# Newton steps of the spectral norms, and two row splits, written for GpSimd instead of VectorE, in a two-layer FNet and sliding-window attention kernel

## The chip, the cores and the metric

The kernel runs on one core of one Trainium2 chip. The metric is the device time of one execution in microseconds (us), the median of the runs; a lower time is better. PE is TensorE (matmuls), DVE is VectorE, ACT is ScalarE, POOL is GpSimd, SP is the engine that issues most transfers.

## The reference

Four sublayers are applied in turn to a sequence of 2048 rows of 640 numbers: spectral mixing, attention, spectral mixing, attention. Each adds to its input what it computes from the normed input.

```python
x = x + _A_ref(_layernorm(x), dft_seq_re, dft_seq_im, dft_hid_re, dft_hid_im)
x = x + _B_ref(_layernorm(x), wqkv, wo)
...
def _A_ref(x, ...):
    a = jnp.einsum("bsd,ed->bse", x, dft_hid_re)
    b = jnp.einsum("bsd,ed->bse", x, dft_hid_im)
    return jnp.einsum("ts,bse->bte", dft_seq_re, a) - jnp.einsum("ts,bse->bte", dft_seq_im, b)
```

`_B_ref` is attention with 32 heads of 20 and a window of 256 rows, with a projection to q, k and v before it and one after it. `_layernorm` takes the mean off a row and divides by the root of its variance plus 1e-5; it has no weights.

## The kernel before

**Layers and tiles.** The 2048 rows are 16 tiles of 128. `spectral` and `attention` are called once for each of the two layers, spectral first. Numbers for TensorE are kept as two 16-bit floats, a high half and the low half that is left (`hi` and `lo`), and a product is made of three matmuls (high by high, high by low, low by high).

**The spectral sublayer.** Its sequence transform is done in 4 rounds r of 4 row tiles, each of 8 steps j. Before a round, four "z stages" (`z_stage`) transform the round's four row tiles along the hidden axis; they are spread over the steps of the round before. A step j makes the seven products of a Strassen form, in the order m0 (bank x, `main_a`), then m6 (bank z) and m5 (bank y) of the step before (`main_c`), then m1 (y), m2 (x), m4 (z) and m3 (y) (`main_b`). A product is 12 matmuls. DVE adds the result of a product to the residual tiles (`add`, L559); the second product in a PSUM bank (m3 after m1, m6 after m4, m5 after m3) can begin only when DVE has read what the first left there. POOL adds the parts that are shared by two residual quarters: L579 after m0, L589 after m1, L600 after m3. For the next step, `take_c` makes four sums of the matrix's quarters on POOL (L525 to L528), ACT makes seven high halves (L533) and DVE the seven low halves (L536).

**Norms.** `norm_steps` norms a list of row tiles: two BN_STATS and a BN_AGGR a tile give mean and variance (L139, L142), L148 and L149 make a first guess of the inverse root, three Newton steps refine it (L151, L152, two instructions of one number a row each), and with `act` L156 makes the bias and ACT the normed row (L164). Then a split makes the high half on ACT (L177) and the low half (L178) on the engine that is given. In `spectral` norms stand in two places. `side_norm` norms one row tile for a later z stage, 12 tiles a layer, with its split on POOL. `finish(0, 1)` and `finish(1, 1)` norm the first two pairs of row tiles for the attention that follows, near the end of the last round, with their splits on DVE; the normed rows of a pair are transposed by TensorE (four groups of five, `transposed`, copied out by ACT and by DVE in turn), and the projections of the first pair are made among the last products of the round (`ahead`).

**What sets the order.** These norms are generators: `tick`, which is called after every product, runs the next pair of high and low halves and then one step of each generator to its next `yield`. A scheduler then orders every engine's instructions by the order of the program and by when it reckons that their inputs and buffers are free; each engine works through its own list in that order. Matmuls have two banks for x, y, z and for `pf` (transposes, projections), the sums of the matrix three buffers.

```python
            def tick(cut=True):
                if splits and cut:
                    with behind():
                        for f in splits.pop(0):
                            f()
                with behind():
                    for g in list(side):
                        if next(g, None) is None:
                            side.remove(g)
```

Of the kernel before, what the change touches and what calls it, by code (L numbers as in the profile page):

```python
# [13 lines left out]
I32 = mybir.dt.int32  # L14
AF = mybir.ActivationFunctionType
OP = mybir.AluOpType
# [38 lines left out]
ROOT = float(0x5F3759DF - (1 << 22) - (1 << 30))  # L55
# [8 lines left out]
X_UP = 2.0 ** 10  # L64
# [8 lines left out]
def body(ctx: ExitStack, tc: tile.TileContext, x_in, cmat, whid, wqkv, wo, out):  # L73
    nc = tc.nc
# [42 lines left out]
    normed = [None]  # L117
# [11 lines left out]

    matmul, transpose = partial(tensor, "matmul"), partial(tensor, "transpose")  # L130

    def norm_steps(xs, ys, act=False):

        n = len(xs)
        mv = keep.tile([P, n, 2], F32, tag=f"lnmv{n}", name="lnmv", bufs=2)
        for k, x in enumerate(xs):
            st = keep.tile([P, 2, 6], F32, tag="lnst", name="lnst", bufs=2)
            for h in range(2):
                nc.vector.bn_stats(st[:, h], x[:, h * 320:(h + 1) * 320])  # L139
                if h == 0:  # L140
                    yield
            nc.vector.bn_aggr(mv[:, k], st.rearrange("p a b -> p (a b)"))  # L142
            yield
        t = keep.tile([P, 3, n], F32, tag=f"lnt{n}", name="lnt", bufs=2)
        ts = nc.vector.tensor_scalar
        for k in range(n):
            h, g, u = (t[:, m, k:k + 1] for m in range(3))
            ts(h, mv[:, k, 1:2], 1e-5, -0.5 * X_UP ** -2, op0=OP.add, op1=OP.mult)  # L148
            ts(g.bitcast(I32), h.bitcast(I32), -0.5, ROOT, op0=OP.mult, op1=OP.add)  # L149
            for m in range(3):  # L150
                ts(u, g, g, h, op0=OP.mult, op1=OP.mult)  # L151
                normed[0] = ts(g, u, 1.5, g, op0=OP.add, op1=OP.mult).ins  # L152
                if m == 0:
                    yield
            if act:
                normed[0] = ts(u, mv[:, k, 0:1], g, -1.0, op0=OP.mult, op1=OP.mult).ins  # L156
            yield
        for _ in range(2 if act else 0):
            yield
        for k, x in enumerate(xs):  # L160
            g, u = t[:, 1, k:k + 1], t[:, 2, k:k + 1]
            y = keep.tile([P, D], F32, tag="lny", name="lny", bufs=2)
            if act:
                nc.scalar.activation(y, x, AF.Identity, bias=u, scale=g)  # L164
            else:
                normed[0] = ts(y, x, mv[:, k, 0:1], g, op0=OP.subtract, op1=OP.mult).ins
            ys.append(y)
            yield

    def layer_norm(xs):  # L170
        ys = []
        for _ in norm_steps(xs, ys):
            pass
        return ys

    def split(hi, lo, y, eng):
        nc.scalar.activation(hi, y, AF.Copy)  # L177
        eng.tensor_tensor(lo, y, hi, op=OP.subtract)  # L178
# [3 lines left out]
    def load(out, in_):  # L182
        with ExitStack() as order:
            if in_turn[0] and loads:
                order.enter_context(tc.issue_after(loads[-1]))
            elif floor:
                order.enter_context(tc.issue_after(floor[-1]))
            i = nc.sync.dma_start(out, in_)
        loads.append(i.ins)
# [189 lines left out]
    def spectral(layer, res_src, hidden, first):  # L379
        with ExitStack() as st:  # L380
# [47 lines left out]
            def transposed(xs, k, xt):  # L428
                pt = new_f().bitcast(F16)[:, :ND * P].rearrange("p (a b) -> p a b", a=ND)
                for dt in range(ND):  # L430
                    transpose(pt[:, dt], xs[:, k, dt * P:(dt + 1) * P], idh)
                if k:
                    nc.vector.tensor_copy(xt[:, k], pt)
                else:
                    nc.scalar.activation(xt[:, k], pt, AF.Copy)
# [3 lines left out]
            def load_x(s):  # L439
                x = sb.tile([P, D], F32, tag="xin", name="xin", bufs=NXIN)  # L440
                load(x, res_src[s])
                return x

            def split_x(s, y, eng):
                XS[s] = keep.tile([P, 2, D], F16, tag="xs", name="xs", bufs=2)
                split(XS[s][:, 0], XS[s][:, 1], y, eng)
# [36 lines left out]
            def side_norm(s):  # L483
                x, ys = load_x(s), []
                for _ in range(3):
                    yield 1
                for _ in norm_steps([x], ys, True):
                    yield 1
                split_x(s, ys[0], nc.gpsimd)
                yield 1  # L490
# [140 lines left out]
            def finish(j, pace):  # L631
                xs = [sb.tile([P, D], F32, tag="xin", name="x2", bufs=NXIN) for k in range(2)]
                for k in range(2):
                    load(xs[k], x2_d[2 * j + k])
                for _ in range(3):
                    yield 1
                ys, xss = [], []
                for _ in norm_steps(xs, ys, True):
                    for _ in range(pace):
                        yield 1  # L640
                for y in ys:
                    xs = keep.tile([P, 2, D], F16, tag="xs", name="xs", bufs=2)
                    split(xs[:, 0], xs[:, 1], y, nc.vector)
                    xss.append(xs)
                    yield 1
                for _ in range(2):
                    yield 1
                proj.new_rows(j)
                for k, xs in enumerate(xss):
                    for m in range(2):  # L650
                        transposed(xs, m, proj.rows[j][0][:, k])
                        yield 1
                    finished[0] += 1
# [79 lines left out]
            if first:  # L733
                constants()
                x = [load_x(s) for s in range(2)]
                f = [load_w(n) for n in range(NXIN - 2)]
                norm_x(0, x[:1], nc.vector)
                for n in range(10):
# [5 lines left out]
                    if n == 7:  # L744
                        x = [load_x(s) for s in range(2, 4)]
# [3 lines left out]
            for r in range(NR):  # L749
                for k in range(RS if r == 0 else 0):  # L750
                    s = RS * r + k
                    if first:
                        if s == 1:
                            norm_x(2, x, nc.gpsimd)
                            marks["dve"] = normed[0]
                        if s:
                            turned_x(s)
                        if k < RS - 1:
                            turn_x(s + 1, 2)
                    elif s > 1:  # L760
                        hidden.fetch(s)
                    if r == 0 and k == 1:
                        load_c(1)
                        with behind() as order:
                            if not first:
                                order.enter_context(tc.issue_after(hidden.after))
                            take_c(0)
                    if first and k == RS - 1:
                        side.append(side_norm(RS))
                    if first or s > 1:  # L770
                        z_stage(s)
                if r == NR - 1:
                    proj = Projections()
                for j in range(NJ):
                    n = r * NJ + j
# [35 lines left out]
                    if r < NR - 1 and j in STAGES[r]:  # L811
                        k = STAGES[r].index(j)
# [629 lines left out]
```

## Time and profile before

| what | value |
|---|---|
| median of 3 runs | 2056.11 us (2054.0 to 2058.06) |
| profiled execution, its own time | 2055.16 us |
| span of its profile | 2053.4 us |
| PE busy | 1987.5 us (97%) |
| DVE busy | 1563.3 us (76%) |
| POOL busy | 1469.2 us (72%) |
| ACT busy | 1115.0 us (54%) |
| granted TensorE clock, mean | 0.996 of full speed |

The span is that of the instructions; 1.76 us of the execution's own time lie around it. The first spectral layer takes about the first 555 us of it, the second about 1060 to 1565 us; the attention layers follow each. In a row of the timeline stand start, duration, engine, line, operation, output<-inputs, shape, count, and in brackets the engine's idle time before the row with what ended it; rows of equal neighbours are merged and overlap their successor by the pipeline's tail. In a row of the waits stand total, times and longest, in us.

### The profile page before, as it was taken

What the parts mean: (1) busy time and instruction counts of PE and PEld (TensorE: products, weight loads), DVE (VectorE), ACT (ScalarE), POOL (GpSimd) and SP (SyncE); (2) the same over time, 40 slices, a digit from 0 to 9 for tenths busy, and PEclk for the clock granted to TensorE, in tenths of its full rate; (3) what the DMA queues carried; (4) which work ended last, traced back from release to release, by engine and by line L of the source; (5) the groups of instructions that cost most, each with busy time, mean ns of one, the idle gap of its engine ahead of it and who ended that gap; (6) DMA issues with size and microseconds to landing.
All of it is one profiled execution on the core that took longest, in us unless ns stands there. A gap on an engine that the chain in (4) does not pass through costs nothing.

```text
span 2053.4 us, 55784 instructions
## 1 busy us (share of the span) xinstructions
PE 1987.5 (97%) x21881; PEld 1449.1 (71%) x21881; DVE 1563.3 (76%) x3261; ACT 1115.0 (54%) x1973; POOL 1469.2 (72%) x2162
## 2 busy tenths in 40 slices
PE   6999999999999999999999999999999999999998
PEld 4777777776767777777667777777677677777765
DVE  8888778768688888777638779787777788887682
ACT  5544555533347677666654444444332567766674
POOL 5777788877557788776557778777783677777653
PEclk9999999999999999999999999999999999999999
DMA  7556566566544444434535565454844455443222
GB/s 274 178 197 202 175 209 228 179 240 216 154 108 111 121 122 121 103 85 111 158 132 179 171 165 186 147 174 139 300 148 131 99 118 123 124 120 98 76 68 72
DMA packets 280508, 311.10 MB, mean 152 GB/s; under 512 B 107572, under 2 KB 214836, under 8 KB 271156
## 3 DMA queue, kind: packets, MB, share of 16 engines
q1 hardware_dynamic: 279668, 306.88, 50.2%
q8 instruction: 171, 2.80, 0.6%
q14 instruction: 93, 0.76, 0.1%
q10 hardware_dynamic: 576, 0.66, 0.1%
HBM read 201.72 MB, written 83.46 MB: 139 GB/s over the span
## 4 chain that ended last, share of the span: by engine, by line
PE 68%; DVE 16%; issue 5%; POOL 4%; ACT 4%; DMA 3%; SPq 0%; DVEq 0%; ACTq 0%; POOLq 0%
PE pf L126 32%; PE y L126 10%; PE x L126 10%; PE z L126 7%; PE sk L126 5%; DVE cc L536 4%; PE sq L126 3%; DVE sq L1156 2%; DVE m L1158 2%; DMA res<-accd 2%; ACT ptq L1212 2%; DVE lnst L139 1%; DVE res L559 1%; DVE lnt L151 1%; POOL cs L526 1%
## 5 line engine op out<-in xcount | busy, mean ns | idle before, releaser
L126 PEld LDWEIGHTS <-cc 128*128 128x128 f16 x5376 | 524.4, 98 | 214.4 <-issue 14.7
L1212 ACT ACTIVATE ptq<-sk,shift,alpha 128x768 f32<-128x768 f32 (+2 forms) x512 | 471.9, 944 | 125.9 <-PE sk L126 74.7
L126 PEld LDWEIGHTS <-big 128*128 128x128 f16 x4320 | 414.3, 98 | 129.3 <-issue 24.2
L1158 DVE TENSOR_REDUCE m<-sq 128x2 f32<-128x512 f32 (+1 forms) x512 | 345.5, 675 | 19.1
L533 ACT ACTIVATE cc<-cs 128x512 f16<-128x512 f32 x256 | 153.6, 624 | 261.4 <-POOL cs L526 150.4
L126 PE MATMUL pf<-early,big 128*128 128x256 f16 x2400 | 292.8, 276 | 0.1
L126 PE MATMUL y<-zc,cc 128*128 128x320 f16 x1728 | 262.8, 299 | 3.2 <-DVE pf L559 3.2
L1216 POOL TENSOR_SCALAR_AFFINE_SELECT ptq<-ptq 128x512 f32<-128x512 f32 x224 | 142.1, 634 | 172.5 <-ACT ptq L1212 171.4
L536 DVE SCALAR_TENSOR_TENSOR cc<-cs,cc 128x512 f16<-128x512 f32 x256 | 248.0, 978 | 6.9 <-ACT cc L533 6.8
L1156 DVE COPY_PREDICATED sq<-mask,sk 128x256 f32<-128x256 int32 x448 | 189.5, 423 | 53.4 <-PE sq L126 51.7
L536 DVE SCALAR_TENSOR_TENSOR cc<-cq,cc 128x512 f16<-128x512 f32 x192 | 205.5, 1072 | 0.1
L126 PE MATMUL pf<-ptq,v 128*32 128x128 f32 (+1 forms) x3840 | 184.4, 330 | 5.1 <-DVE x L935 2.7
L126 PE MATMUL z<-zc,cc 128*128 128x320 f16 x1152 | 177.7, 299 | 6.6 <-DVE res L559 6.6
L1218 POOL TENSOR_SCALAR_AFFINE_SELECT ptq<-ptq 128x512 f32<-128x512 f32 x256 | 164.8, 644 | 18.8 <-ACT ptq L1212 18.6
L126 PE MATMUL x<-zc,cc 128*128 128x320 f16 x1152 | 177.7, 299 | 0.0
L365 ACT ACTIVATE qf<-pf 128x256 f32<-128x256 f32 x160 | 61.1, 382 | 163.7 <-PE pf L126 112.4
L126 PEld LDWEIGHTS pf<-ptq,v 128*32 128x32 f32 x3840 | 110.9, 110 | 48.4 <-DVE x L935 3.9
L126 PE MATMUL pf<-big,early 128*128 128x320 f16 x960 | 141.4, 300 | 0.0
L525 POOL TENSOR_TENSOR cs<-cq 128x512 f32<-128x512 f32 x64 | 86.7, 1355 | 69.5 <-DVE cc L536 68.8
L126 PEld LDWEIGHTS <-qs 62*128 62x128 f16 x2688 | 90.1, 94 | 56.6 <-issue 53.1
L126 PE MATMUL pf<-bo,ot 128*128 128x320 f16 x840 | 123.8, 299 | 2.1 <-DVE big L286 1.2
L126 PE MATMUL x<-big 128*128 128x320 f16 x825 | 122.3, 299 | 2.0 <-DVE big L425 2.0
(142 smaller groups left out, 3481.6 us busy)
## 6 DMA issues: line engine op xcount, KB each, us to landing
cq<-in_cmat_dram SPq DMA_DIRECT2D x64, 1024.0 KB
accd<-res SPq DMA_DIRECT2D x96, 320.0 KB
res<-accd SPq DMA_DIRECT2D x96, 320.0 KB
x<-x2d SPq DMA_DIRECT2D x64, 320.0 KB
qkd<-early SPq DMA_DIRECT2D x160, 128.0 KB
ks<-qkd SPq DMA_DIRECT2D x108, 160.0 KB
qs<-qkd SPq DMA_DIRECT2D x84, 160.0 KB
x2d<-res SPq DMA_DIRECT2D x32, 320.0 KB
```

The lines of the kernel that those rows point to most:

```text
L126: i = getattr(nc.tensor, what)(*args, **kw)
L139: nc.vector.bn_stats(st[:, h], x[:, h * 320:(h + 1) * 320])
L151: ts(u, g, g, h, op0=OP.mult, op1=OP.mult)
L365: nc.scalar.activation(f, pf[:, :QB], AF.Copy, scale=down)
L525: g.tensor_tensor(s1, a21, a22, op=OP.add)
L533: nc.scalar.activation(cc[m][:, 0], f, AF.Copy, scale=C_UP)
L536: nc.vector.scalar_tensor_tensor(cc[m][:, 1], f, C_UP, cc[m][:, 0], op0=OP.mult, op1=OP.subtract)
L1156: marks["dve"] = nc.vector.copy_predicated(near[pi][:, :, 0], mask[:, None, :].to_broadcast([P, 2, P]), far).ins
L1158: marks["dve"] = nc.vector.tensor_reduce(TOP[n][:, pi, :, k], near[pi][:, :, :1 + (i >= 1)], axis=AX.XY, op=OP.max).ins
L1212: marks["act"] = nc.scalar.activation(o[:, pi], tps[pi][:, :, first:], AF.Sigmoid, bias=shift, scale=alpha[:, 0:1]).ins
L1216: nc.gpsimd.affine_select(out=q[:, :, a0], in_=q[:, :, a0], pattern=[[0, 4], [-1, P]], base=0, channel_multiplier=1, compare_op=OP.is_gt, ...
L1218: ins = nc.gpsimd.affine_select(out=q[:, :, a0 + 2], in_=q[:, :, a0 + 2], pattern=[[0, 4], [1, P]], base=0, channel_multiplier=-1, compare ...
```

## The change

`norm_steps` gets an argument `roots`. Where it is given, VectorE still makes the statistics and the first guess, the guess in two instructions for all tiles of the list at once, and the six Newton instructions a tile and the bias are written for that engine, in four steps of the generator. `side_norm` and `finish` give GpSimd. A list of one tile takes 10 steps to its normed row instead of 7, a list of two 13 instead of 12. The low halves in `finish` are written for GpSimd too. Other norms stay as they were.

```diff
-    def norm_steps(xs, ys, act=False):
+    def norm_steps(xs, ys, act=False, roots=None):
...
-        for k in range(n):
+        if roots is not None:
+            h, g = t[:, 0], t[:, 1]
+            ts(h, mv[:, :, 1], 1e-5, -0.5 * X_UP ** -2, op0=OP.add, op1=OP.mult)
+            ts(g.bitcast(I32), h.bitcast(I32), -0.5, ROOT, op0=OP.mult, op1=OP.add)
+            yield
+            ts = roots.tensor_scalar
+            for m in range(3):
+                for k in range(n):
+                    h, g, u = (t[:, j, k:k + 1] for j in range(3))
+                    ts(u, g, g, h, op0=OP.mult, op1=OP.mult)
+                    normed[0] = ts(g, u, 1.5, g, op0=OP.add, op1=OP.mult).ins
+                yield
+            for k in range(n if act else 0):
+                normed[0] = ts(t[:, 2, k:k + 1], mv[:, k, 0:1], t[:, 1, k:k + 1], -1.0, op0=OP.mult, op1=OP.mult).ins
+            yield
+        for k in range(0 if roots is not None else n):
...
-                for _ in norm_steps([x], ys, True):
+                for _ in norm_steps([x], ys, True, nc.gpsimd):
...
-                for _ in norm_steps(xs, ys, True):
+                for _ in norm_steps(xs, ys, True, nc.gpsimd):
...
-                    split(xs[:, 0], xs[:, 1], y, nc.vector)
+                    split(xs[:, 0], xs[:, 1], y, nc.gpsimd)
```

Lines after the change lie 15 further down from L163 on (L559 is L574, L525 is L540, L579 is L594, L589 is L604, L600 is L615, L178 is L193); the Newton lines are L155 and L156, the bias L159.

On DVE, where the first pair is normed in the first layer (`finish(0, 1)`), these rows stand one after the other before; `lnt` holds guess and factors, `res<-z` and `pf<-y` are the adds that free the banks z and y, `cc<-cs` is a low half of the matrix:

```order
L559 SCALAR_TENSOR_TENSOR res<-z,res 128x320
L152 TENSOR_SCALAR lnt<-lnt 128x1
L149 TENSOR_SCALAR lnt<-lnt 128x1
L536 SCALAR_TENSOR_TENSOR cc<-cs,cc 128x512
L151 TENSOR_SCALAR lnt<-lnt 128x1 x2
L152 TENSOR_SCALAR lnt<-lnt 128x1 x2
L151 TENSOR_SCALAR lnt<-lnt 128x1 x2
L152 TENSOR_SCALAR lnt<-lnt 128x1 x2
L156 TENSOR_SCALAR lnt<-lnmv,lnt 128x1
L151 TENSOR_SCALAR lnt<-lnt 128x1
L559 SCALAR_TENSOR_TENSOR pf<-y,pf 128x320
```

The same place on DVE after the change:

```order
L574 SCALAR_TENSOR_TENSOR res<-x,res 128x320
L142 BN_AGGR lnmv<-lnst 128x2
L551 SCALAR_TENSOR_TENSOR cc<-cq,cc 128x512
L148 TENSOR_SCALAR lnt<-lnmv 128x2
L574 SCALAR_TENSOR_TENSOR res<-z,res 128x320
L149 TENSOR_SCALAR lnt<-lnt 128x2
L551 SCALAR_TENSOR_TENSOR cc<-cs,cc 128x512
L574 SCALAR_TENSOR_TENSOR pf<-y,pf 128x320
```

Between the adds `res<-z` and `pf<-y` ten Newton instructions and a bias are gone, and of the guess one instruction for both tiles is left.

On POOL at this place, before; `cs` are the sums of the matrix's quarters for the next step, `res<-res,pf` the shared adds:

```order
L528 TENSOR_TENSOR cs<-cq,cs 128x512
L589 TENSOR_TENSOR res<-res,pf 128x320
L579 TENSOR_TENSOR res<-res,pf 128x320
L600 TENSOR_TENSOR res<-res,pf 128x320
L525 TENSOR_TENSOR cs<-cq 128x512
L527 TENSOR_TENSOR cs<-cq 128x512
L526 TENSOR_TENSOR cs<-cs,cq 128x512
L579 TENSOR_TENSOR res<-res,pf 128x320
L528 TENSOR_TENSOR cs<-cq,cs 128x512
L589 TENSOR_TENSOR res<-res,pf 128x320
L600 TENSOR_TENSOR res<-res,pf 128x320
```

On POOL at this place, after, from the same L579 (now L594) on:

```order
L594 TENSOR_TENSOR res<-res,pf 128x320
L155 TENSOR_SCALAR lnt<-lnt 128x1 x2
L156 TENSOR_SCALAR lnt<-lnt 128x1 x2
L155 TENSOR_SCALAR lnt<-lnt 128x1 x2
L156 TENSOR_SCALAR lnt<-lnt 128x1 x2
L155 TENSOR_SCALAR lnt<-lnt 128x1 x2
L156 TENSOR_SCALAR lnt<-lnt 128x1 x2
L159 TENSOR_SCALAR lnt<-lnmv,lnt 128x1 x2
L615 TENSOR_TENSOR res<-res,pf 128x320
L540 TENSOR_TENSOR cs<-cq 128x512
```

The fourteen small instructions stand in one piece between two shared adds, ahead of the next step's sums. A little further down POOL's list, after the sums, the two splits (`xs<-lny,xs`) follow:

```order
L543 TENSOR_TENSOR cs<-cq,cs 128x512
L193 TENSOR_TENSOR xs<-lny,xs 128x640
L594 TENSOR_TENSOR res<-res,pf 128x320
L604 TENSOR_TENSOR res<-res,pf 128x320
L193 TENSOR_TENSOR xs<-lny,xs 128x640
L615 TENSOR_TENSOR res<-res,pf 128x320
```

The first split stands ahead of the shared adds L594 and L604, the second between L604 and L615. On PE the four groups of transposes of the first pair stand one product later than before (the first one behind product m6 instead of ahead of it), those of the second pair two products later, and the first pair's ten projections one product later; all other matmuls keep their order.

More of the change, by code (lines that the diff above doesn't have):

```diff
@@ L165, in norm_steps @@
             else:
-                normed[0] = ts(y, x, mv[:, k, 0:1], g, op0=OP.subtract, op1=OP.mult).ins
+                normed[0] = nc.vector.tensor_scalar(y, x, mv[:, k, 0:1], g, op0=OP.subtract, op1=OP.mult).ins
             ys.append(y)
```

## The prediction

> **What bounds the kernel now.** I read the busy times first (the table above: PE is busy 97% of the span), then the waits of PE by stretch of the span, then the stretches with the waits in the timeline of each engine. The first spectral layer, without its start and its end (50 to 440 us), has among the waits of PE:
>
> ```profile
> PE y L126 <- DVE pf L559: 1.4, 2, 0.8
> PE pf L126 <- POOL xs L178: 1.0, 1, 1.0
> ```
>
> That is next to nothing in 390 us: there PE itself is the bound, and whatever another engine saves is hidden. At the end of the last round, 440 to 500 us in the first layer and 1440 to 1500 us in the second, the waits are these:
>
> ```profile
> PE z L126 <- DVE res L559: 3.2, 3, 1.6
> PE y L126 <- DVE pf L559: 1.6, 1, 1.6
> ...
> PE z L126 <- DVE res L559: 3.4, 3, 1.6
> PE y L126 <- DVE pf L559: 1.6, 1, 1.6
> ```
>
> In 60 us of each layer PE stands still 4.8 and 5.0 us, always for an add on DVE that has to read a bank first. The table of stretches shows why (columns: length, PE, PE loads, DVE, ACT, POOL busy, clock, DMA):
>
> ```profile
> 470.00:480.00 10.00, 7.36 (x54) 5.07 (x52) 10.00 (x33) 6.63 (x11) 5.77 (x5) 1.00 0.71 264
> 480.00:490.00 10.00, 8.37 (x69) 6.09 (x67) 10.00 (x12) 5.00 (x9) 8.97 (x7) 1.00 0.53 174
> ```
>
> DVE has no idle moment, POOL has over 4 us in the first of the two. The timeline of PE gives the three waits of the first layer that fall into this stretch:
>
> ```profile
> 472.57 1.79 PE L126 MATMUL z<-zc,cc 128*128 128x320 f16 x12 [1.05 <-DVE res L559]
> 475.95 3.42 PE L126 MATMUL y<-zc,cc 128*128 128x320 f16 x24 [1.59 <-DVE pf L559]
> ...
> 487.80 1.79 PE L126 MATMUL z<-zc,cc 128*128 128x320 f16 x12 [1.64 <-DVE res L559]
> ```
>
> **The change part by part.** *Handover, first pair, DVE.* The timeline of DVE between the adds that PE waits for:
>
> ```profile
> 472.04 0.48 DVE L559 SCALAR_TENSOR_TENSOR res<-z,res 128x320 f32<-128x320 f32 x1
> ...
> 473.88 0.44 DVE L151 TENSOR_SCALAR lnt<-lnt 128x1 f32<-128x1 f32 x2
> ...
> 475.23 0.27 DVE L151 TENSOR_SCALAR lnt<-lnt 128x1 f32<-128x1 f32 x1
> 475.41 0.48 DVE L559 SCALAR_TENSOR_TENSOR pf<-y,pf 128x320 f32<-128x320 f32 x1
> ...
> 482.38 1.88 DVE L178 TENSOR_TENSOR xs<-lny,xs 128x640 f16<-128x640 f32 x1
> ...
> 485.46 1.89 DVE L178 TENSOR_TENSOR xs<-lny,xs 128x640 f16<-128x640 f32 x1
> 487.27 0.48 DVE L559 SCALAR_TENSOR_TENSOR res<-z,res 128x320 f32<-128x320 f32 x1
> ...
> 490.81 0.48 DVE L559 SCALAR_TENSOR_TENSOR res<-z,res 128x320 f32<-128x320 f32 x1
> ```
>
> The wait of 1.05 ends with the add at 472.04, ahead of which stand statistics and low halves that stay: I leave it whole. The wait of 1.59 ends with the add at 475.41; from 473.88 to there DVE does Newton steps alone, 1.53 us, and one more Newton instruction stands before 473.88. All of that leaves, so this wait goes: 1.59. The wait of 1.64 ends with the add at 487.27, ahead of which stand two splits of 1.88 and 1.89. Without them and the Newton steps DVE is over 5 us earlier there, while PE, 1.59 earlier, asks 3.2 us earlier: this wait goes too, 1.64. That is 3.23 us a layer, and the second layer has the same three waits: 6.5 us.
>
> *Handover, first pair, POOL.* No row shows a Newton step on POOL. The nearest, from the groups of instructions by form (busy us in total, mean ns of one), with what it costs on DVE and what the split costs on both:
>
> ```profile
> L151 DVE TENSOR_SCALAR lnt<-lnt 128x1 f32<-128x1 f32 x192 | 50.8, 269 | 4.1
> L152 DVE TENSOR_SCALAR lnt<-lnt 128x1 f32<-128x1 f32 x192 | 39.6, 211 | 4.0
> L178 DVE TENSOR_TENSOR xs<-lny,xs 128x640 f16<-128x640 f32 x9 | 13.0, 1441 | 0.0
> L1166 POOL TENSOR_SCALAR mf<-m 128x8 f32<-128x8 f32 x128 | 33.8, 264 | 9.4 <-DVE m L1158 6.3 <-DVE lnt L148 2.2 <-PE pf L126 0.3
> L178 POOL TENSOR_TENSOR xs<-lny,xs 128x640 f16<-128x640 f32 x31 | 48.7, 1572 | 34.5 <-ACT xs L177 34.5
> L1435 POOL MEMSET const-float32-1.0<- 128x1 f32 x1 | 0.1, 99 | 0.0
> ```
>
> From below, 99 ns (one number a row, nothing read); from above, twice the dearer DVE row, 538 ns. I take 264 ns: the same operation on POOL with eight numbers a row. Between dependent instructions POOL has a gap, here 0.08 us from the end of the first row to the start of the second:
>
> ```profile
> 568.78 0.19 POOL L1167 CAST tops<-mf 128x8 f16<-128x8 f32 x1
> 569.05 0.21 POOL L1168 TENSOR_TENSOR tops<-mf,tops 128x8 f16<-128x8 f32 x1
> ```
>
> In a pair two tiles alternate, which covers it: 14 x 0.264 = 3.7 us a pair. A single tile pays it: 7 x 0.344 = 2.4 us. POOL at the handover, before:
>
> ```profile
> 472.55 0.86 POOL L579 TENSOR_TENSOR res<-res,pf 128x320 f32<-128x320 f32 x1
> 475.97 1.36 POOL L600 TENSOR_TENSOR res<-res,pf 128x320 f32<-128x320 f32 x1 [2.56 <-DVE pf L559]
> 478.96 1.27 POOL L525 TENSOR_TENSOR cs<-cq 128x512 f32<-128x512 f32 x1 [1.63 <-DVE cc L536]
> ...
> 484.95 1.72 POOL L528 TENSOR_TENSOR cs<-cq,cs 128x512 f32<-128x512 f32 x1
> 486.63 1.44 POOL L589 TENSOR_TENSOR res<-res,pf 128x320 f32<-128x320 f32 x1
> ```
>
> The Newton steps start when L579 ends, at 473.4, and end at 477.1; then L600 to 478.4, and the sums begin at 478.4 instead of 478.96. The two idle pieces of 2.56 and 1.63 us cover them, and the wait for DVE that made the second is shorter. From there POOL works without a pause: four sums (6.3 us, three from 478.96 to L579 at 483.54 and L528) to 484.7, the first split (1.6) to 486.3, L579 and L589 (1 to 1.4 each) to about 488.5. The add `res<-z` that stands at 490.81 takes L589's result, and with PE 3.2 us earlier it would come at 487.6: it waits about 1 us for POOL, a new wait. Behind it on DVE stand a low half, an add, another low half and the copy of the second group of transposes, for whose bank the fourth group waits. That group stands one product later than before, so PE gives it about a product's 1.7 us; I charge 0.5 us a layer, 1.0 in all. The ends: nothing at 99 ns a step, 3.3 us a layer at 470 ns (the average of twice the two DVE rows): 2.9 us more on POOL, passed on.
>
> *Second pair.* POOL is full when its Newton steps come:
>
> ```profile
> 520.00:530.00 10.00, 10.00 (x84) 8.02 (x82) 6.76 (x19) 4.37 (x10) 9.76 (x13) 1.00 0.27 81
> ```
>
> They push the last four projections' halves back, after them their stores and the loads of the first stacks, which the scores take:
>
> ```profile
> 541.59 6.19 SPq L188 DMA_DIRECT2D ks<-qkd  x6
> ...
> L126 PE MATMUL sq<-ks x24: 212/216/227, 555.5 to 564.9; 62*128 62x128 f16 x24
> ```
>
> The last load is issued by 547.8 and first used at 555.5. With POOL 2 to 3 us later and PE 2.7 earlier, about 2 us are left for it to land: cost nothing, up to 1 us a layer if a step is dear. The splits of this pair come where POOL waits for DVE anyway, and are taken off a DVE that PE did not wait for: nothing.
>
> *The 24 single tiles.* DVE loses 3 x (0.269 + 0.211) + 0.211 = 1.65 us each, hidden behind PE: a gain of up to the 1.4 above in the first layer, taken as none. POOL gets 2.4 us each. Its densest part in the first layer:
>
> ```profile
> 300.00:400.00 100.00, 99.51 (x751) 72.03 (x749) 86.26 (x146) 54.33 (x100) 92.06 (x68) 1.00 0.62 207
> ```
>
> Three tiles are normed in it: 7.2 us into 7.9 us of idle time. Locally POOL will run 2 or 3 us late; a product's add may come two products (3.4 us, the row of 24 matmuls above) after it before PE waits, so I charge 0.3 us, and for the second layer nothing. The three more steps before a normed row bring it nearer to its use; the tightest is the transpose with the wait of 1.0 above, at 73 us. There POOL stands idle just when the Newton steps come,
>
> ```profile
> 62.80 1.24 POOL L600 TENSOR_TENSOR res<-res,pf 128x320 f32<-128x320 f32 x1 [3.65 <-DVE pf L559]
> ```
>
> and 2.4 us fit into 3.65: nothing. Without that cover it is up to 2.4 us, once.
>
> *A rule against the change.* The split costs 1572 ns on POOL and 1441 on DVE, 9% more. The Trainium skill (GPSIMD Engine Reference, Engine selection) says that elementwise work belongs on VectorE, GpSimd being about twice as slow with two inputs. In these rows it is not, beside each other's traffic; by the rule the two splits of the first pair would take 5.8 us on POOL, and 1.3 us more would come through a layer, 2.5 us less gain. I go by the row.
>
> **The sum.** 6.5 - 1.0 - 0.3 = 5.2 us. The profiled execution took 2055.16 us (span 2053.4, 1.76 around it): 2050.0. It lies 0.95 below the median of the three runs, so against the median, 2056.1 - 5.2 = 2050.9 us. What a measurement of this kernel can tell from no change is about 0.2%, 4.1 us.
>
> **The rivals.** (1) *POOL eats half of the gain.* Steps with operands read by row cost more on DVE (269 and 211 against its plain ones), and if they cost 0.35 to 0.4 us on POOL a pair takes 1.2 to 1.9 us more, all of which arrives at the add `res<-z`: 2.0 a layer instead of 0.5, and 0.5 us more in the single tiles. Gain 2 to 3, time 2053.5. For it: the full POOL from 478.96 on; against it: nothing else was late there. Chance 25%.
>
> (2) *POOL becomes the bound: slower.* Mechanism: at 470 ns a step the single tile takes 3.3 us and the pair 6.6. The handover then gives back 3.3 a layer, so nothing is gained; the loads of the stacks come 1 us late in each layer, 2 us; and from 320 to 400 us, with the three tiles' 10 us in 7.9 of idle time, mostly before and after where they are wanted, POOL runs up to 7 us late, 4 more than PE lets pass. Together 6 us more: 2062. It decides from about 0.45 us a step. It is what the rule above would make of the Newton steps, read for the small ones too. For it: 92% in that stretch; against it: the 264 ns of a like instruction. Chance 12%.
>
> (3) *All goes, and more*: steps near 0.1 us, no wait for POOL, the 1.05 partly gone and the 1.4 too: 6.5 + 0.4 + 1.4 = 8.3, time 2047.8. Chance 8%.
>
> That the change does not do what it says can be left out: the order shows the steps gone from between the adds.
>
> **How the numbers follow.** The forecast keeps 55%; its own range is 2048.5 (no wait for POOL) to 2052.5 (1.3 a layer). The range reaches over (1) and most of (3): 2047 to 2056.5. Faster by over 0.2% means under 2052.0: the forecast but for its end, and (3): 58%. Within 0.2%: that end and (1): 30%. Slower: (2), 12%.
>
> **What would show it.** Right: PE's waits for DVE between 470 and 490 us, and at the same place of the second layer, down from 4.3 to about 1 us; the Newton steps on POOL near 264 ns, in its idle time before L600; a new short wait of DVE's `res<-z` for POOL and of the fourth transposes for DVE's copy. Wrong: Newton rows of 400 ns or more, waits of PE that lead through POOL (late sums, late shared adds) between 320 and 400 or 480 and 530 us, scores that wait for the first stacks, or PE waits that stay as long for another reason.

## The result, and the profile after

The changed kernel is slower: 2081.47 us (median of 4 runs, 2078.09 to 2085.37) against 2056.91 us, ratio 1.0129 with a 95% interval of 1.0113 to 1.0144; of 2055 us that is 26.5 us (the two medians differ by 24.6). The profiled execution took 2080.09 us (span 2078.4), 25 us more than that of before.

Where the 25 us lie is read from the same matmuls in both kernels. These are rows of the views of single tiles (count, shortest/median/longest ns, start of the first and of the last in us), of before and then of after. The `sq<-ks` products are the first scores behind each layer's handover (those of the first layer first, those of the second last), `z<-big` opens the second layer, and the last `y<-early` stands in that layer's last rounds.

```profile
L126 PE MATMUL sq<-ks x192: 212/216/227, 555.5 to 1614.7; 62*128 62x128 f16 x192
...
L126 PE MATMUL z<-big x120: 297/299/474, 11.9 to 1075.0; 128*128 128x320 f16 x120
...
L126 PE MATMUL y<-early,cc x576: 296/299/299, 55.4 to 1446.6; 128*128 128x320 f16 x192
```

```profile
L126 PE MATMUL sq<-ks x192: 212/216/227, 562.3 to 1640.7; 62*128 62x128 f16 x192
...
L126 PE MATMUL z<-big x120: 297/299/474, 11.9 to 1084.6; 128*128 128x320 f16 x120
...
L126 PE MATMUL y<-early,cc x576: 296/299/299, 55.5 to 1463.8; 128*128 128x320 f16 x192
```

The first scores start 6.8 us later (562.3 against 555.5), and the second layer 9.6 later. Then 7.6 us more are lost in its rounds (17.2 at `y<-early`), and 8.8 more by its last such score (26.0). The large losses are in three kinds of places: the handovers, the scores right behind them, and, as the waits show next, the start of the second layer. A smaller one is among the single tiles of the first layer: from 50 to 440 us PE waits 6.6 us where before it waited 4.5. At the start of the first handover the layer is 1.9 us late (the product ahead of its first wait starts at 471.58 against 469.73); but e1_splits below, whose norms up to there are those of before, has 471.27, so most of this can be a difference between two executions.

Of the waits of PE in the changed kernel (us in total, times, longest), these are the three largest of which before had none:

```profile
PE x L126 <- DMA big<-xs: 6.6, 1, 6.6
...
PE pf L126 <- ACT early L450: 5.3, 2, 2.7
PE sq L126 <- DMA x2d<-res: 4.9, 2, 2.9
```

The first is the single one at the start of the second layer; the other two come once in each layer, at the projections of the handover and at the scores. The waits that were to go, at 475.95 and 487.80 us of before, answer to these rows of PE's timeline:

```profile
474.92 1.79 PE L126 MATMUL z<-zc,cc 128*128 128x320 f16 x12 [1.54 <-ACT cc L548]
487.65 1.79 PE L126 MATMUL z<-zc,cc 128*128 128x320 f16 x12 [1.16 <-DVE res L574]
491.53 1.79 PE L126 MATMUL y<-zc,cc 128*128 128x320 f16 x12 [1.81 <-DVE pf L574]
503.50 2.49 PE L126 MATMUL pf<-early,big 128*128 128x256 f16 x15 [2.67 <-ACT early L450]
565.40 0.27 PE L126 MATMUL sq<-ks 62*128 62x128 f16 x3 [2.90 <-DMA x2d<-res]
```

The 1.54 stands where before had 1.05. The wait of 1.59 is gone: behind 474.92 there is none until 487.65. From there to the first scores four stand, 8.5 us together, where before had one of 1.64 at the handover. Newton's steps on GpSimd, from the groups by form (busy us, mean ns of one):

```profile
L155 POOL TENSOR_SCALAR lnt<-lnt 128x1 f32<-128x1 f32 x96 | 50.0, 523 | 8.9 <-DVE lnt L149 3.9
L156 POOL TENSOR_SCALAR lnt<-lnt 128x1 f32<-128x1 f32 x96 | 34.5, 362 | 7.2
L159 POOL TENSOR_SCALAR lnt<-lnmv,lnt 128x1 f32<-128x1 f32 x32 | 9.2, 290 | 2.4
```

The forecast had 264 ns for each. They are 224 instructions of 418 ns in the mean (93.7 us), and at the handover of the first layer the timeline of POOL shows them dearer:

```profile
475.39 1.54 POOL L155 TENSOR_SCALAR lnt<-lnt 128x1 f32<-128x1 f32 x2
...
481.65 0.50 POOL L159 TENSOR_SCALAR lnt<-lnmv,lnt 128x1 f32<-128x1 f32 x2
...
482.93 1.26 POOL L540 TENSOR_TENSOR cs<-cq 128x512 f32<-128x512 f32 x1
...
488.29 1.85 POOL L193 TENSOR_TENSOR xs<-lny,xs 128x640 f16<-128x640 f32 x1
...
496.09 1.72 POOL L540 TENSOR_TENSOR cs<-cq 128x512 f32<-128x512 f32 x1
```

The pair takes from 475.39 to 482.15, 6.8 us where the forecast had 3.7. The sums of the first weights begin at 482.93 (forecast 478.4), and the next weights' sums at 496.09 (493.32 before). From 475 to 505 us POOL is busy for 29.7 of the 30 us. Who passes that on is seen on ACT and DVE. First the two waits at 487.65 and 491.53:

```profile
481.94 0.92 ACT L179 ACTIVATE lny<-x,lnt 128x640 f32<-128x640 f32 x1 [7.05 <-POOL lnt L159]
```

```profile
483.41 3.78 DVE L551 SCALAR_TENSOR_TENSOR cc<-cq,cc 128x512 f16<-128x512 f32 x1 [1.29 <-ACT cc L548]
490.99 0.49 DVE L574 SCALAR_TENSOR_TENSOR pf<-y,pf 128x320 f32<-128x320 f32 x1 [2.11 <-POOL res L594]
```

ACT's normalising instruction waits 7.05 us for the end of Newton's steps, and high halves stand behind it. VectorE's low half waits for one of them, takes 3.78 us beside POOL's work, and the add `res<-z` at 487.12, for which PE waits 1.16 us, comes behind it. The add `pf<-y` waits for the shared add L594, which stands behind the first split on POOL, and PE waits 1.81 us for it. Then the copy of the transposed rows on ACT:

```profile
497.84 0.63 ACT L548 ACTIVATE cc<-cs 128x512 f16<-128x512 f32 x1 [6.39 <-POOL cs L540]
501.19 1.15 ACT L548 ACTIVATE cc<-cs 128x512 f16<-128x512 f32 x2 [2.72 <-POOL cs L541]
...
502.76 0.68 ACT L450 ACTIVATE early<-pf 128x640 f16<-128x640 f16 x1
```

ACT works in order. High halves of the next weights wait for POOL's sums, and the copy of the transposed rows (L450), for whose input nothing is missing any more, stands behind them. It ends at 503.44, and PE's projections at 503.50 wait for it. The place in ACT's queue has its part in this. In the kernel before the copy stood behind the first of these high halves (495.08), and now it stands behind all four:

```profile
495.61 0.69 ACT L435 ACTIVATE early<-pf 128x640 f16<-128x640 f16 x1
```

The start of the second layer, GpSimd's first split there and SyncE's first transposing load, of before and then of after (timelines of POOL and SP), with PE's wait:

```profile
1095.83 1.40 POOL L178 TENSOR_TENSOR xs<-lny,xs 128x640 f16<-128x640 f32 x1 [0.26 <-ACT xs L177]
1097.26 1.36 SPq L196 DMA_TRANSPOSE big<-xs  x1
```

```profile
1117.65 1.39 POOL L193 TENSOR_TENSOR xs<-lny,xs 128x640 f16<-128x640 f32 x1
1119.08 1.36 SPq L211 DMA_TRANSPOSE big<-xs  x1
1122.49 3.75 PE L126 MATMUL x<-big 128*128 128x320 f16 x15 [6.58 <-DMA big<-xs]
```

The layer runs 9.6 us late there, but the split comes 21.8 us later. Newton's steps stand before it, and by the three more steps of a single tile it moved behind the next product's shared adds and sums (how much each costs is told apart by e6_dve below).

At the scores, the last loads of the first stacks are issued by 559.7 us (552.48 and 7.26) where before they were issued by 547.8:

```profile
552.48 7.26 SPq L203 DMA_DIRECT2D ks<-qkd  x6
```

Last, PE's own speed. The same 21881 matmuls have 1993.0 us of busy time where before had 1987.5. In the table of stretches (columns as before; the clock is the third number from the right) slow stretches stand behind the new long waits:

```profile
503.50:506.50 3.00, 3.00 (x18) 2.24 (x18) 1.15 (x1) 0.38 (x1) 1.89 (x3) 0.66 0.85 284
506.50:509.50 3.00, 3.00 (x21) 2.11 (x19) 0.00 (x0) 0.87 (x3) 1.40 (x3) 0.77 0.30 109
...
1122.00:1125.00 3.00, 2.51 (x10) 1.48 (x11) 0.00 (x0) 0.00 (x0) 2.60 (x6) 0.50 0.93 347
```

Behind the wait of 2.67 us the granted clock is 0.66 and 0.77 for two stretches of 3 us, which loses 3 x 0.34 + 3 x 0.23 = 1.7 us on top of the wait. Behind the one of 1.81 at 491.53 it stays at 1.00 (494 to 500 us). Of the 25 us, 5.5 are longer matmuls, which goes with the slower clock (0.993 in the mean against 0.996), and 19.5 are idle time.

### The profile page after: what moved, and what is told of

Same layout as the page of the kernel before. It is cut to its first block, busy times and chain, and to the rows that moved or that the text cites. A ratio compares the mean times of both kernels' runs of the same rounds, so it can differ in the third digit from the quotient of the medians.

```text
span 2078.4 us, 55790 instructions
## 1 busy us (share of the span) xinstructions
PE 1993.0 (96%) x21881; PEld 1450.7 (70%) x21881; DVE 1514.9 (73%) x3021; ACT 1115.5 (54%) x1973; POOL 1563.6 (75%) x2394
## 4 chain that ended last, share of the span: by engine, by line
PE 60%; DVE 9%; POOL 4%; issue 3%; ACT 3%; DMA 2%; SPq 0%; DVEq 0%; ACTq 0%; POOLq 0%
PE pf L126 31%; PE x L126 8%; PE y L126 8%; PE sk L126 5%; PE z L126 5%; PE sq L126 3%; DVE sq L1171 2%; DVE m L1173 2%; ACT ptq L1227 2%; DMA res<-accd 1%; DVE cc L551 1%; POOL lnt L155 1%; DVE lnst L139 1%; POOL cs L541 1%; DVE lnt L166 1%
## 5 line engine op out<-in xcount | busy, mean ns | idle before, releaser
L126 PEld LDWEIGHTS <-cc 128*128 128x128 f16 x5376 | 524.8, 98 | 218.3 <-issue 17.9
L551 DVE SCALAR_TENSOR_TENSOR cc<-cs,cc 128x512 f16<-128x512 f32 x256 | 252.9, 1003 | 36.2 <-ACT cc L548 36.0
L551 DVE SCALAR_TENSOR_TENSOR cc<-cq,cc 128x512 f16<-128x512 f32 x192 | 199.7, 1041 | 2.8 <-ACT cc L548 2.6
L574 DVE SCALAR_TENSOR_TENSOR res<-z,res 128x320 f32<-128x320 f32 x128 | 62.2, 486 | 93.3 <-PE z L126 70.7
```

Of the source, the lines that this page charges most:

```text
L126: i = getattr(nc.tensor, what)(*args, **kw)
L551: nc.vector.scalar_tensor_tensor(cc[m][:, 1], f, C_UP, cc[m][:, 0], op0=OP.mult, op1=OP.subtract)
L574: marks["dve"] = nc.vector.scalar_tensor_tensor(o, z, Y_DOWN, f, op0=OP.mult, op1=OP.add).ins
```

## The experiments

Three theories were told apart. Theory 1: the work of Newton's steps makes GpSimd late, and all that queues behind it. Theory 2: the order, by the three more steps of a single tile. Theory 3: the splits. The differences in us below are ratio less 1, times 2055; the plain differences of the medians lie up to some 2 us off them.

**e1_splits.** Only the splits move.

```
# before
-                    split(xs[:, 0], xs[:, 1], y, nc.vector)
+                    split(xs[:, 0], xs[:, 1], y, nc.gpsimd)
```

> The kernel before, with only the lower halves of the first two pairs moved to GpSimd; Newton's steps stay on VectorE in their old places. Theory 1 (GpSimd is full because of the 224 small Newton instructions, which took 443 ns each in the mean, and everything queued behind them comes late): two more splits of 1.6 us at a handover do little, -2 to +4 us against before, 2055 to 2061. Theory 2 (the three more steps of a single tile push the splits, loads and transposes behind other work): no change, 2055 to 2058. Theory 3 (the splits themselves make GpSimd late at the handover): most of the handovers' 14 us is lost, 2067 or more.

Measured: 2055.81 us against 2054.92, ratio 1.0001 (0.9990 to 1.0012). The splits alone cost nothing, and gain nothing either, although VectorE is rid of them. PE's timeline and POOL's show why:

```profile
491.13 0.45 PE L126 MATMUL pf<-idh,xs 128*128 128x128 f16 x5 [1.88 <-POOL xs L178]
```

```profile
487.96 1.31 POOL L589 TENSOR_TENSOR res<-res,pf 128x320 f32<-128x320 f32 x1
489.22 3.65 POOL L178 TENSOR_TENSOR xs<-lny,xs 128x640 f16<-128x640 f32 x2
```

The wait of 1.64 us for VectorE has gone; PE now waits 1.88 us for the split itself, which comes at 489.22 at the end of GpSimd's queue.

**e2_newton.** The changed kernel with the splits back on VectorE.

```
# after
-                    split(xs[:, 0], xs[:, 1], y, nc.gpsimd)
+                    split(xs[:, 0], xs[:, 1], y, nc.vector)
```

> The changed kernel with only the splits of the first two pairs back on VectorE; Newton's steps stay on GpSimd. Theory 1: nearly all of the loss stays, 2072 to 2082. Theory 2: the loss of about 8 us at the start of the second layer stays, the rest is open, 2066 to 2080. Theory 3: the handovers come back, 2062 to 2070.

Measured: 2076.89 us, ratio 1.0102 (1.0085 to 1.0118), 21 us. Theory 3 falls: without the splits on GpSimd four fifths of the loss stay. The time lies in the range of theory 1, but in that of theory 2 as well; the next run tells those two apart.

**e3_order.** The changed kernel with Newton's steps on VectorE, in the steps of the change.

```
# after
-                for _ in norm_steps([x], ys, True, nc.gpsimd):
+                for _ in norm_steps([x], ys, True, nc.vector):
...
-                for _ in norm_steps(xs, ys, True, nc.gpsimd):
+                for _ in norm_steps(xs, ys, True, nc.vector):
```

> The changed kernel with Newton's steps on VectorE, in exactly the steps that the change gives them (three more for a single tile, one more for a pair), and the splits on GpSimd. Only the engine of the 224 instructions differs from the changed kernel. Theory 1: the loss goes, 2050 to 2060. Theory 2: the late splits at the start of the second layer stay, 2064 to 2074. Theory 3: the handovers' loss stays, 2067 to 2075, with the start of the second layer undisturbed.

Measured: 2065.91 us, ratio 1.0044 (1.0029 to 1.0059), 9 us. Against the changed kernel only the engine of 224 instructions differs, and that is 17.5 us of the 26.5. The time lies in the range that theory 2 gave; theory 1 alone would have been at 2060 or less. So the engine makes the larger part of the loss, and something is left for the order. PE's timeline shows one part: with the splits on GpSimd and the pair's transposes later, the copy on ACT is late even so, and PE waits longer for it than the 2.67 us of the changed kernel.

```profile
499.08 1.80 PE L126 MATMUL pf<-early,big 128*128 128x256 f16 x15 [3.68 <-ACT early L450]
```

So this wait doesn't come from the price of Newton's steps on GpSimd. The profiles of this run and of the changed kernel, whose spans differ by 17.5 us too, show where that price arrives. At the two handovers (440 to 550 and 1430 to 1560 us) PE waits 6.7 us each here, and 7.2 and 8.2 in the changed kernel. The scores wait for no load here, and 4.9 us there; the start of the second layer waits 3.0 and 6.6; the single tiles of the first layer (50 to 440 us) 3.2 and 6.6; and the matmuls are 2.5 us longer there. The rest is spread.

**e6_dve.** As e3_order, with the splits on VectorE too (both edits above): only the order is left.

> As the run before it, with the splits back on VectorE too: of the change only the order of the steps (and the first guess made once for both tiles of a pair) is left. Theories 1 and 3: as the kernel before, 2053 to 2059. Theory 2: 2064 to 2074.

Measured: 2059.70 us, ratio 1.0015 (1.0005 to 1.0025), 3.1 us, between what the theories gave. The order costs something, less than theory 2 needs. Its largest new wait is at the start of the second layer:

```profile
1109.70 3.88 PE L126 MATMUL x<-big 128*128 128x320 f16 x15 [3.03 <-DMA big<-xs]
```

So of the 6.58 us there, 3.03 come from the order and the rest from Newton's time on GpSimd: in the new order the wait is 3.0 in both runs with Newton's steps of the single tiles on VectorE (e3_order and this one) and 6.6 in e2_newton, e5_singles and e11_copies, which have them on GpSimd; in e4_pairs, with the old order of the single tiles, there is none. From e6_dve by e3_order to the changed kernel the loss is split in steps, whose sum is the whole by construction: order 3.1, splits on top of that order 6.0, the engine of Newton's steps 17.5. The other way round, by e2_newton, the engine comes first with 17.9 (21.0 less 3.1) and the splits last with 5.5, so the shares hardly depend on the way. In the old order the same splits cost nothing (e1_splits).

**e4_pairs** and **e5_singles.** The two halves of the change.

```
# after, e4_pairs
-                for _ in norm_steps([x], ys, True, nc.gpsimd):
+                for _ in norm_steps([x], ys, True):
# after, e5_singles
-                for _ in norm_steps(xs, ys, True, nc.gpsimd):
+                for _ in norm_steps(xs, ys, True):
...
-                    split(xs[:, 0], xs[:, 1], y, nc.gpsimd)
+                    split(xs[:, 0], xs[:, 1], y, nc.vector)
```

> The changed kernel with the 24 single tiles back as they were (Newton's steps on VectorE, in their old steps); only the four pairs have their 56 Newton instructions and their splits on GpSimd. Theory 1, with the loss where the trace shows it (about 14 us at the two handovers and the scores behind them, about 8 at the start of the second layer): 2066 to 2071. Rival (the loss goes with the count of instructions moved, and a quarter of them stays): 2058 to 2063.

> The other half: the 24 single tiles with their 168 Newton instructions on GpSimd, the pairs as before (Newton's steps and splits on VectorE, old steps). Theory 1 by places: the wait for the transposing load at the start of the second layer (6.6 us and the slow clock after it) and the 2 to 4 us lost between 330 and 430 us stay, the handovers are as before: 2064 to 2069. Rival (by count): 2072 to 2078.

Measured: e4_pairs 2073.58 us against 2055.68, ratio 1.0098 (1.0075 to 1.0122), 20.1 us; e5_singles 2069.10 us, ratio 1.0066 (1.0051 to 1.0081), 13.6 us. The half with a quarter of the moved instructions makes the larger part. It also has the moved splits, some 6 us by the runs above; the 14 that are left are still as much as the other half costs with three times the instructions, so the place decides more than the count. e4_pairs lies 2.6 us above the upper end that theory 1 gave, e5_singles at it, and together, 33.7 us, they lose more than the whole change; so they hide in one another in part. In the profiles PE's idle time grows by 14.1 and 8.8 us over that of before (19.5 in the whole change) and its busy time by 3.4 and 6.5 (5.5), so over half of the excess there is longer matmuls, which differ with the granted clock; the rest stays open. The wait of the scores for the loads stands in e4_pairs (3.5 us in the first layer) and e2_newton (3.1) and is absent from e5_singles, e3_order and e6_dve: it comes with the pairs' Newton steps on GpSimd.

**e7_steps.** The changed kernel with as many steps as before had.

```
# after
             for m in range(3):
...
                     normed[0] = ts(g, u, 1.5, g, op0=OP.add, op1=OP.mult).ins
-                yield
...
             yield
+            for _ in range(2 * n - 2):
+                yield
```

> The changed kernel with all Newton steps of a tile in one step of the generator, filled up with empty steps to the number that the kernel before has (2 for a single tile, 4 for a pair). The instructions and their engines are those of the changed kernel. Theory 1: only what the order cost by itself comes back, 3 to 9 us: 2072 to 2078. Theory 2 in its last form (GpSimd is late only because the splits stand behind other work): 2062 or less.

Measured: 2117.69 us, ratio 1.0303 (1.0285 to 1.0322), 62 us slower than before, 36 slower than the change. Every theory had expected a gain, and all are wrong on this. The timelines of ACT and PE at the largest wait:

```profile
391.63 0.92 ACT L180 ACTIVATE lny<-xin,lnt 128x640 f32<-128x640 f32 x1 [6.65 <-POOL lnt L158]
...
393.22 0.42 ACT L299 ACTIVATE zc<-x 128x320 f16<-128x320 f32 x1
```

```profile
394.55 1.76 PE L126 MATMUL x<-early,cc 128*128 128x320 f16 x6 [10.14 <-DVE zc L302]
```

GpSimd reaches Newton's steps late, at the end of a full queue (they end at 391.6 us); ACT's normalising instruction waits for them, and behind it stand the copies of PE's products (L299), which PE's next product needs. The idle time of ACT ahead of the 24 single tiles' normalising (the last number of the group) in e6_dve, after and e7_steps:

```profile
L179 ACT ACTIVATE lny<-xin,lnt 128x640 f32<-128x640 f32 x24 | 21.8, 909 | 0.0
```

```profile
L179 ACT ACTIVATE lny<-xin,lnt 128x640 f32<-128x640 f32 x24 | 22.0, 918 | 38.9 <-POOL lnt L159 38.9
```

```profile
L180 ACT ACTIVATE lny<-xin,lnt 128x640 f32<-128x640 f32 x24 | 22.1, 921 | 102.7 <-POOL lnt L158 102.7
```

In the kernel before, with Newton's steps on VectorE, this idle time is 30.1 us. The added steps, over which the change spreads Newton's instructions, are what keeps ACT from waiting longer for GpSimd; with the steps on VectorE they cost 3.1 us (e6_dve), and with them on GpSimd they save 36.

**e8_double.** More work on GpSimd in the same order.

```
# after
                     ts(u, g, g, h, op0=OP.mult, op1=OP.mult)
+                    ts(u, g, g, h, op0=OP.mult, op1=OP.mult)
                     normed[0] = ts(g, u, 1.5, g, op0=OP.add, op1=OP.mult).ins
```

> The changed kernel with the first instruction of each Newton step (u from g, g and h) written twice on GpSimd, which changes no number: 96 more instructions of about 0.52 us, 50 us more work for GpSimd in the same order. Theory 1 (GpSimd's work is what costs): the 94 us that the change added cost 16 to 17 us, and the next 50 find less idle time, so 10 to 20 us more: 2091 to 2102. Rival (the cost is one of places in the queue, not of work): 2080 to 2086.

Measured: 2104.21 us, ratio 1.0239 (1.0222 to 1.0256), 22.6 us more than the change and 2 us above what theory 1 gave. The added instructions' groups come to 40 us, so over half of them reaches the end, where of the change's 94 us a fifth did (17.5). That is theory 1, with the idle time used up.

**e11_copies.** The copies of the pairs' transposes on VectorE.

```
# after
-            def transposed(xs, k, xt):
+            def transposed(xs, k, xt, dve=False):
...
-                if k:
+                if k or dve:
...
-                        transposed(xs, m, proj.rows[j][0][:, k])
+                        transposed(xs, m, proj.rows[j][0][:, k], True)
```

> The changed kernel with all copies of the pairs' transposes on VectorE; in the changed kernel half of them stand on ScalarE behind high halves of the next weights that wait for GpSimd's sums, and TensorE waits 2.67 us for one in each layer, with a slow clock after it. If that queue on ScalarE is the cause of this wait, 2.67 us and about 1.5 for the clock go in each layer: 2071 to 2075. Rival (VectorE's low halves wait for the same high halves, so that its copies come as late): 2079 to 2084.

Measured: 2073.67 us against 2055.33, ratio 1.0089 (1.0073 to 1.0105), 8.2 us less than the change by the ratios, and in the range expected. PE's timeline at these projections, now without a wait, and the stretch behind it:

```profile
501.83 1.80 PE L126 MATMUL pf<-early,big 128*128 128x256 f16 x15
```

```profile
503.00:506.00 3.00, 3.00 (x27) 2.40 (x26) 2.42 (x3) 1.08 (x3) 2.92 (x4) 1.00 0.86 300
```

The wait of 2.67 us is gone and the clock stays at 1.00. That the queue on ACT made this wait is shown. That its end is worth the 8.2 us is not: the profiled execution (2077.25 us, the longest of the four) has a span only 2.9 us below that of the change. In its first layer two waits for the copies on VectorE have come, 1.0 us together, and the scores wait 3.7 us for a transfer instead of 2.9. Nor is the clock part of it shown, since e4_pairs has the same waits of 2.67 us and a clock of 1.00 behind them.

**e9_merged** and **e10_merged_splits.** What the change wanted, a shorter queue on VectorE, got without GpSimd: both tiles of a pair in one instruction.

```
# before, e9_merged
+        if n == 2:
+            h, g, u = (t[:, m] for m in range(3))
...
+            for m in range(3):
+                tt(u, g, g, op=OP.mult)
+                tt(u, u, h, op=OP.mult)
+                normed[0] = stt(g, u, 1.5, g, op0=OP.add, op1=OP.mult).ins
...
+                normed[0] = stt(u, mv[:, :, 0], -1.0, g, op0=OP.mult, op1=OP.mult).ins
...
# e10_merged_splits, beside it
-                    split(xs[:, 0], xs[:, 1], y, nc.vector)
+                    split(xs[:, 0], xs[:, 1], y, nc.gpsimd)
```

> The kernel before with Newton's steps of a pair made for both tiles at once on VectorE: a tensor_tensor for g times g, one for that times h, and a scalar_tensor_tensor for the new g, all on 128x2, in the same four steps of the generator; 12 instructions of a pair in place of 18, none of which reads a number a row from another operand. GpSimd's work stays as it was. If VectorE's full queue at the handover is what TensorE waits for there (9.8 us in both layers by the profile of before), the 2 us less work of a pair take 2 to 3 us of a layer's 4.9 away: 2050 to 2053. Rival (the waits lie on the other work of VectorE there): no change, 2054 to 2057.

> The run before it with the splits of the first two pairs on GpSimd, too. With the splits alone VectorE lost two instructions of 1.9 us at the handover and the time did not change, since a wait for the split on GpSimd (1.88 us) came in place of the one for VectorE. The same is expected here: within 2 us of the run before it. Rival (both together free VectorE enough to let the handover run through): 2047 to 2050.

Measured: e9_merged 2051.86 us against 2055.33, ratio 0.9983 (0.9971 to 0.9995); e10_merged_splits 2050.87 us, ratio 0.9976 (0.9966 to 0.9986), 4.9 us faster than before and 31 faster than the change. Both are where they were expected. The intervals of the two overlap; what the splits add here is not settled, and the interval of e9_merged ends close to 1. The waits of PE from 440 to 520 us, first e9_merged, then e10_merged_splits:

```profile
PE z L126 <- DVE res L574: 3.4, 2, 2.7
PE z L126 <- ACT cc L548: 1.5, 1, 1.5
```

```profile
PE z L126 <- ACT cc L548: 1.5, 1, 1.5
PE pf L126 <- DVE early L448: 1.0, 2, 0.6
PE y L126 <- DVE pf L574: 0.9, 1, 0.9
PE pf L126 <- POOL xs L193: 0.4, 1, 0.4
PE z L126 <- DVE res L574: 0.2, 1, 0.2
```

Once Newton's steps are short, the splits on GpSimd take the longest wait for VectorE (2.7) away and bring one of 0.4 for themselves, beside others of 1.0 and 0.9: 4.0 us in the whole. In e9_merged the waits there come to 4.9 us, as before (4.8), in an execution of 2056.59 us, above its median. So its gain is measured in time, but that it comes from this handover is not shown.

## Why the prediction was wrong

Forecast: 2050.9 us, 2047.0 to 2056.5. The rival that POOL becomes the bound had the sign (12%), and priced it at 2062.

- *"this wait goes: 1.59"*: right. No wait stands there in the changed kernel.
- *"this wait goes too, 1.64"*: wrong. Where only the splits leave VectorE (e1_splits) the add is early enough, but PE needs what the split makes and waits 1.88 for it instead. In the changed kernel 1.16 for the add stays: the low half before it is held by ACT, which waits for the end of Newton's steps, and takes 3.78 us. The forecast took the queue that got shorter and left out when the moved instructions themselves would end. Gain of the splits alone: none.
- *"I take 264 ns: the same operation on POOL with eight numbers a row"*: the first step that failed. Measured 418 in the mean, and 6.8 us a pair instead of 3.7. The rival's 6.6 us a pair, at 470 ns a step, was met almost to the number at this handover; the mean of all 224 lies under its "about 0.45 us a step". The rule of the Trainium skill (GPSIMD Engine Reference, Engine selection: about twice as slow with two inputs) was weighed and set aside on the row of the split, 9% dearer; for Newton's steps the ratio to VectorE is 523/269 and 362/211, 1.9 and 1.7. In e3_order, with these steps on VectorE, 17.5 us of the loss are gone.
- *"I charge 0.5 us a layer"* for the new wait for POOL: an add on DVE waits 2.11 us for POOL's shared add, and PE 1.81. And the chain was followed on DVE alone. The sums of POOL also feed ACT, and ACT's queue holds the copy of the transposes: 2.67 us a layer (e11_copies). That wait stands with Newton's steps on VectorE too (3.68 in e3_order, 1.0 in e6_dve): it comes from the later place of the copy and from the splits.
- Second pair, *"cost nothing, up to 1 us a layer if a step is dear"*: the loads of the stacks came late as the rival had it, and PE waits for them 2.9 and 2.0 us.
- *"The three more steps before a normed row bring it nearer to its use"*, charged with nothing: the forecast read one place of the first layer, where PE transposes. In the second layer the rows go through a transposing load, and there 6.58 us were lost, 3.03 of them by order alone (e6_dve). With the splits moved as well the order costs 9 us (e3_order), which the sum had at nothing.
- Not in the sum at all: matmuls that take 5.5 us longer in the whole, which goes with the lower granted clock.

Theory 1 holds as the larger part: 17.5 us go with the engine of the 224 instructions. Theories 2 and 3 fell as the main cause; order and splits together make the other 9 us. Open is how the losses of pairs and single tiles hide in each other, and why the splits cost nothing in the old order and 6 us in the new.

## What to carry to other kernels

Work moved to an engine that is full at that place delays everything queued behind it, and its readers pass the delay on through their own in-order queues: list for each reader what stands behind the instruction that will wait, on every engine, before taking the new wait as small. A moved instruction has to be timed twice, by the place it leaves and by the moment at which its own result is ready. Where a queue is too long, fewer and wider instructions on the same engine (12 for a pair in place of 18) gained 3.5 us (e9_merged) where moving them lost 26.5.

## What the runs showed of the hardware

A small instruction on GpSimd has two prices. A row of DVE and the one of POOL beside it, in the changed kernel:

```profile
1108.28 0.68 DVE L551 SCALAR_TENSOR_TENSOR cc<-cs,cc 128x512 f16<-128x512 f32 x1
```

```profile
1108.39 0.79 POOL L155 TENSOR_SCALAR lnt<-lnt 128x1 f32<-128x1 f32 x1
```

Of the single rows of L155, the 13 with nothing on DVE beside them, the 11 beside an add L574 alone and the 15 beside a combination L301 alone took 0.34 us each; the 10 beside a low half L551 alone took 0.69 to 1.30, 0.98 in the mean. The low half reads two operands from SBUF (`cs` or `cq`, and `cc`), the adds one from SBUF and one from PSUM. The Trainium skill (SBUF — State Buffer, Who interferes with whom) says that a VectorE instruction with two inputs in SBUF contends with one of GpSimd that reads SBUF, and that one with at most one such input, outside the two-port modes, does not; these rows agree. This contention was the larger part of what the price of 264 ns missed: 0.34 to the mean of 0.523 us in L155, against 0.264 to 0.34.

PE's granted clock does not follow from the length of the wait before it alone. In the changed kernel it fell to 0.66 behind a wait of 2.67 us and to 0.50 behind one of 6.58, and stayed at 1.00 behind one of 1.81. But in e4_pairs it stayed at 1.00 behind both waits of 2.67, and in e3_order behind one of 3.68 us (499 to 514 us); and in the kernel before it was 0.54 from 581 to 584 us, behind waits of 1.52 and 1.00. The Trainium skill (TensorE: Matmul & The Clock Gate, HAM oscillation) warns of idle gaps above some 3.4 us; here shorter ones had a slow clock behind them, and one that was longer had not. What decides is not shown.
